# Steps of weight pieces and of tokens drawn apart, four places for small products, a shorter lag of the second product

## The chip, the cores and the metric

The kernel runs on one core of a Trainium2 chip. The core has TensorE (PE, matmuls, with its weight loads shown apart as PEld), VectorE (DVE), ScalarE (ACT), GpSimd (POOL) and SyncE (SP, which issues most DMAs). Each engine works off its own queue in order. The metric is the device time of one execution in microseconds (us); of the kernel before, three runs have a median of 1328.83 us (1327.54 to 1329.64).

## The reference

Three stages follow each other. Attention over 2 x 768 tokens with 8 heads gives 1536 rows of 512. A mixture of 8 experts sends each row to one expert. A second, dense mixture sends every row through all experts:

```python
def _moe2_ref(x, w_gate, w1, w2):          # x 1536 x 512, w1 8 x 512 x 1024, w2 8 x 1024 x 512
    logits = x @ w_gate
    logits = logits - logits.max()
    P = np.exp(logits)
    for _ in range(8):
        P /= P.sum(1, keepdims=True) + 1e-09
        P /= P.sum(0, keepdims=True) + 1e-09
        P *= N / E
    out = np.zeros((N, D), dtype=np.float32)
    for e in range(E):
        h = np.maximum(x @ w1[e], 0.0)
        out += P[:, e:e + 1] * (h @ w2[e])
```

## The kernel before

*Stages in time.* Attention ends at about 125 us of the trace, the top-1 mixture runs to about 330 us in blocks of 256 sorted rows, and the dense mixture takes the rest, from 346.86 us (its first product) on.

*The dense mixture.* There are 24 units: 8 experts times 3 groups of 512 tokens (`CHUNKS`). Both products are block products of 2 x 2 blocks that are made from 7 smaller products of sums of blocks. A number is split in a high and a low f16 part and multiplied in three matmuls. `first(u, fc, i)` (L1201) does the i-th of the seven small products of a chunk of hidden columns, 6 matmuls into one bank `fx` or `fa`; ACT takes the result (`take`, L1223) and DVE adds (L1226). When a chunk's seven are through, `operands2` (L1244) makes the second product's operands: ACT casts hh (L1256, L1268), DVE makes hl (L1259, L1271) and four sums (L1262 to L1265). `second(e, k, s, i)` (L1286) does one of its seven small products, 12 matmuls into `gx` or `ga`, and adds to the output rows `acc` (L1323, L1331, L1339).

*Weights.* An expert has 8 pieces (class `Piece`, L663): 4 of each weight. A piece is loaded in a buffer `raw` (three of them), its scale is measured (`measure`: ACT's Square with a sum, L691, and a DVE copy `sqb`, L692), PE sums it over the partitions and DVE makes a power of two of it (`rate`, L697, L627, L630), POOL makes sums of blocks (`sums` L705, `sum4` L709), and ACT and DVE write the high and low parts: `raw_hi` and `raw_lo` of the three blocks as they are, `sum_hi` and `sum_lo` of the four sums (L713, L718). The pieces of the first expert are prepared beside the blocks of the top-1 mixture, one step of the list that `plain` returns at a time.

*Tokens.* `tokens(j)` (L1027) makes the dense stage's operands for a pair of row tiles: `load`, `turn` (PE transposes, ACT copies), `operands` (L1063, four sums on DVE, five casts on ACT, five subtractions on DVE or POOL, in one go) and `logits`, a small product. `mixing` (L1098) makes the gates and the eight normalisations. Small products (the scale of a piece, logits, mixing) go to one bank of the pool `pz`.

*The order.* From the first unit on, the program's order is written out. Time is counted in ticks; a unit has 28, an expert 84. `at(tick, f)` puts a step into a plan. The loop at the end goes over the ticks, calls the steps planned for it, then a first product if one is due, and then at times a second product, as a credit in matmul columns allows, `LAG` of it behind the end of the unit. All engines get their instructions in that order. Loads, measures and rates of pieces stand at fixed distances in ticks (`load + 5`, `load + 8`, `begin + 4`).

Of the kernel before, what the change touches and what calls it, by code (L numbers as in the profile page):

```python
# [108 lines left out]
def body(ctx: ExitStack, tc: tile.TileContext, q, k, v, wg1, w1a, w2a, wg2, w1b, w2b, cst, out):  # L109
# [553 lines left out]
    class Piece:  # L663
# [23 lines left out]
        def measure(self, junk):  # L687
            o = own[id(self.raw)]; assert o is self, (self.e, self.second, self.j, o.e, o.second, o.j)
            ssq_, sqb_ = ssq[self.x][:, self.i : self.i + 1], sqb[self.x][:, self.i : self.i + 1]
# [157 lines left out]
    if True:  # L847
# [112 lines left out]
        def plain(i, p):  # L960
# [3 lines left out]
            return [lambda: p.load(raw), idle, idle, lambda: p.measure(junk), p.rate, lambda: (p.raw_hi(), p.sums()), lambda: (p.raw_lo(), p.sum4()),  # L964
# [33 lines left out]
    pz = ctx.enter_context(tc.tile_pool(name="pz", bufs=1, space=PSUM))  # L998
    ps_small.append((pz, "m"))
# [27 lines left out]
    def tokens(j):  # L1027
# [35 lines left out]
        def operands():  # L1063
            t4 = tmp[1].rearrange("p (k t) -> p k t", k=2 * KC)
            c1, c2 = ps
            b11, b21, b12, b22 = c1[:, :K2], c1[:, K2:], c2[:, :K2], c2[:, K2:]
            s1, s2, s3, s4 = (t4[:, i * K2 : (i + 1) * K2] for i in range(4))
# [4 lines left out]
            nc.vector.scalar_tensor_tensor(out=s3, in0=s2, scalar=-1.0, in1=b11, op0=ALU.mult, op1=ALU.subtract)  # L1072
            parts((T1, T2), t4[:, : 2 * K2], nc.vector)
            parts((B22,), b22, nc.vector)
            parts((T3, T4), t4[:, 2 * K2 :], nc.gpsimd if j else nc.vector)
            nc.scalar.copy(bh, b12)
# [19 lines left out]
        return load, turn, operands, logits  # L1096
# [104 lines left out]
    def first(u, fc, i):  # L1201
# [84 lines left out]
    def second(e, k, s, i):  # L1286
# [4 lines left out]
        if i == 0:  # L1291
            gs["x"] = pg.tile([P, DM], F32, tag="x", name="gx")
        if i == 1:
            gs["a"] = pg.tile([P, 2, Q], F32, tag="a", name="ga", bufs=1)
# [35 lines left out]
        if i in (2, 4) or e == E - 1:  # L1330
# [3 lines left out]
            if e == E - 1 and i in (4, 6):  # L1334
                nc.sync.dma_start(out=out[t * P : (t + 1) * P], in_=acc[:, t])
# [14 lines left out]
    pairs[0][0]()  # L1350
    pairs[1][0]()
    warm(pz, "m", 70)
    for i in (1, 2):
        pairs[0][i]()
        pairs[1][i]()
    for j, ticks in enumerate(((2,), (4,), (0, 3, 6, 20), (1, 12, 15, 24), (20, 33, 36, 48), (21, 42, 45, 52))):
        for tick, f in zip(ticks, pairs[j][-len(ticks) :]):
            at(tick, f)
    turns = [76 + t + 5 * i for i in range(8) for t in (-3, 0)]
    for tick, f in zip([52, 54, 58, 62, 66] + turns + [115], mix):  # L1360
# [5 lines left out]
    for e in range(1, E):  # L1366
        s = TICKS * CHUNKS * e
        p1, p2, level = weights(e)
        if e == 1:
            jobs += [(s - 37, p2[0], -99, True), (s - 36, p1[0], s - 15, True), (s - 32, p1[1], s - 8, True), (s - 12, p1[2], s - 1, True)]  # L1370
            jobs += [(s - 6, p1[3], s + 6, False), (s + 1, p2[1], -99, False), (s + 9, p2[3], -99, False), (s + 14, p2[2], -99, False)]
            for p, i, load, square, rate in ((p1[3], 1, -23, -19, -16), (p2[3], 0, -23, -16, -12), (p2[1], 1, -18, -13, -10), (p2[2], 0, -15, -9, -6)):
                at(s + load, lambda p=p, i=i: p.load(spare[i]))
                at(s + square, lambda p=p: p.measure(acc[:, 3].bitcast(BF16)))
                at(s + rate, p.rate)
        else:
            jobs += [(s - 70, p2[3], None, True), (s - 58, p2[0], s - 45, True), (s - 52, p2[1], s - 45, True), (s - 45, p2[2], s - 45, True)]
            jobs += [(s - 32, p1[0], s - 15, True), (s - 26, p1[3], None, True), (s - 19, p1[1], s - 8, True), (s - 13, p1[2], s - 1, True)]
# [8 lines left out]
    free = [47] * len(raws)  # L1387
    for want, p, begin, measure in sorted(jobs, key=lambda x: x[0]):
# [4 lines left out]
        if measure:  # L1393
            junk = raws[i][:, 4:6].rearrange("p a f -> p (a f)").bitcast(BF16)
            at(load + 5, lambda p=p, junk=junk: p.measure(junk))
            at(load + 8, p.rate)
            assert load + 8 <= s - 3, (p.e, p.second, p.j, load - s)
            end = load + 5
        if begin is not None:
            at(load + 6, p.sums)  # L1400
            if p.second and p.j == F2 - 1:
                last[p.e] = p
                end = s + 34
# [71 lines left out]
```

## Time and profile before

| | |
|---|---|
| median of 3 runs | 1328.83 us |
| profiled execution, and its span | 1334.16 us, 1332.4 us |
| PE, DVE, ACT, POOL busy | 1210.5, 1012.3, 853.5, 396.9 us |
| mean granted clock of PE | 0.969 |

The page's busy table is an average over three stages that differ. The span by slices of a fortieth (33 us each) shows this: a digit is the tenth of a slice in which the engine was busy, and PEclk the tenth of full speed that PE was granted:

```profile
PE   6898897998779779999999999999999999999997
DVE  6784766785586888979788787978978787886773
PEclk8898899999889999999999999999999999999999
```

The fourth to the tenth digit are the top-1 mixture, from the eleventh on it is the dense one. The busy time there is to be read stage by stage, and the waits with it.

### The profile page before, as it was taken

The page shows a single profiled execution, that of the slowest core. Times are in us where ns is not written, and L with a number is a line of the kernel's source. Part 1 is how long each engine was busy: PE and PEld are TensorE (multiplying, and loading weights), DVE is VectorE, ACT ScalarE, POOL GpSimd, SP SyncE. Part 2 cuts the span into 40 slices and gives each one's busy share as a digit, 9 for nine tenths or more (in the row PEclk, how much of TensorE's full clock was granted, in tenths as well). Part 3 has the DMA queues.
Part 4 walks back from the last instruction along what each step waited for, and adds up shares of the span by engine and source line. Part 5 has one row for each costly group of instructions (what it writes and reads, how often), then busy time and mean ns, then how long its engine had stood idle before and what let it go on. Part 6 is the DMA issues. An engine that isn't in the chain of part 4 may idle for free.

```text
span 1332.4 us, 27638 instructions
## 1 busy us (share of the span) xinstructions
PE 1210.5 (91%) x10551; PEld 1061.8 (80%) x10551; DVE 1012.3 (76%) x1793; ACT 853.5 (64%) x1599; POOL 396.9 (30%) x450
## 2 busy tenths in 40 slices
PE   6898897998779779999999999999999999999997
PEld 5776786887658668888888888888888888888886
DVE  6784766785586888979788787978978787886773
ACT  5685566665465746767776676677767767765440
POOL 4352434411212221332333242333334324331000
PEclk8898899999889999999999999999999999999999
DMA  9945776765422423343564544346445444643201
GB/s 197 207 85 177 236 252 203 229 196 166 145 86 94 124 79 104 87 128 91 132 151 108 131 118 124 92 121 151 112 127 127 121 97 109 151 112 84 76 33 48
DMA packets 176732, 173.58 MB, mean 130 GB/s; under 512 B 32768, under 2 KB 147840, under 8 KB 176208
## 3 DMA queue, kind: packets, MB, share of 16 engines
q1 hardware_dynamic: 163024, 143.75, 37.8%
q0 software_dynamic: 13568, 27.99, 10.9%
q8 instruction: 85, 1.39, 0.4%
q14 instruction: 55, 0.45, 0.1%
HBM read 136.10 MB, written 15.53 MB: 114 GB/s over the span
## 4 chain that ended last, share of the span: by engine, by line
PE 41%; DVE 11%; issue 5%; ACT 4%; POOL 2%; DVEq 0%; POOLq 0%; ACTq 0%
PE gx L1301 12%; PE fx L1216 11%; PE ga L1301 10%; PE fa L1216 8%; DVE w2l L718 2%; DVE hl L1271 2%; ACT hh L1268 2%; POOL raw L705 1%; DVE c L1263 1%; DVE w1l L718 1%; DVE hl L1259 1%; ACT w2h L713 1%; DVE c L1264 1%; DVE c L1265 1%; DVE acc L1331 1%
## 5 line engine op out<-in xcount | busy, mean ns | idle before, releaser
L1216 PEld LDWEIGHTS <-w1h 128*128 128x128 f16 x2688 | 261.0, 99 | 90.7 <-issue 56.3
L1301 PEld LDWEIGHTS <-hh 128*128 128x128 f16 x2688 | 264.7, 99 | 48.7 <-issue 16.6
L1216 PE MATMUL fx<-xh,w1h 128*128 128x256 f16 x736 | 202.3, 275 | 23.6 <-ACT c L1223 18.2
L1301 PE MATMUL gx<-w2h,hh 128*128 128x256 f16 x768 | 210.4, 274 | 10.2 <-DVE acc L1323 6.3
L705 POOL TENSOR_TENSOR raw<-raw 128x256 f32<-128x256 f32 x192 | 181.7, 960 | 103.3 <-ACT raw L691 92.3
L1301 PE MATMUL gx<-w2l,hh 128*128 128x256 f16 x768 | 210.5, 274 | 0.0
L1301 PE MATMUL gx<-w2h,hl 128*128 128x256 f16 x768 | 210.5, 274 | 0.0
L1216 PE MATMUL fx<-xl,w1h 128*128 128x256 f16 x736 | 202.7, 275 | 1.4 <-POOL xl L1061 1.4
L1216 PE MATMUL fx<-xh,w1l 128*128 128x256 f16 x736 | 202.9, 276 | 0.0
L1223 ACT ACTIVATE c<-fx,kap 128x256 f32<-128x256 f32 x288 | 131.9, 471 | 73.0 <-PE fx L1216 64.6
L1301 PE MATMUL ga<-w2h,hh 128*128 128x256 f16 x576 | 158.4, 275 | 4.9 <-DVE acc L1331 4.9
L1301 PE MATMUL ga<-w2l,hh 128*128 128x256 f16 x576 | 158.5, 275 | 0.0
L1301 PE MATMUL ga<-w2h,hl 128*128 128x256 f16 x576 | 158.4, 275 | 0.0
L1216 PE MATMUL fa<-xh,w1h 128*128 128x256 f16 x552 | 151.9, 275 | 4.4 <-ACT c L1223 4.4
L1216 PE MATMUL fa<-xl,w1h 128*128 128x256 f16 x552 | 151.8, 275 | 0.0
L1216 PE MATMUL fa<-xh,w1l 128*128 128x256 f16 x552 | 151.7, 275 | 0.0
L1216 PEld LDWEIGHTS <-w1l 128*128 128x128 f16 x1344 | 132.8, 99 | 18.6 <-issue 1.6
L1301 PEld LDWEIGHTS <-hl 128*128 128x128 f16 x1344 | 132.4, 99 | 16.1
L1271 DVE TENSOR_TENSOR hl<-c,hh 128x1024 f16<-128x1024 f32 x96 | 124.5, 1297 | 27.1 <-ACT hh L1268 27.0
L709 POOL TENSOR_TENSOR raw<-raw 128x256 f32<-128x256 f32 x64 | 58.3, 910 | 199.9 <-issue 104.4
L1268 ACT CAST hh<-c 128x1024 f16<-128x1024 f32 x96 | 99.8, 1039 | 23.2 <-DVE c L1265 22.0
L1339 ACT ACTIVATE y<-gx,pws 128x256 f32<-128x256 f32 x144 | 67.9, 472 | 69.7 <-PE gx L1301 51.1
(257 smaller groups left out, 2648.0 us busy)
## 6 DMA issues: line engine op xcount, KB each, us to landing
raw<-in_moe_w SPq DMA_DIRECT2D x64, 512.0 KB, 4.3
raw<-in_moe_w SPq DMA_DIRECT2D x228, 128.0 KB, 3.7
xh<-xohd SPq DMA_DIRECT2D x147, 128.0 KB, 2.6
xl<-xold SPq DMA_DIRECT2D x147, 128.0 KB, 2.9
acc<-y POOLq DMA_DIRECT2D x72, 256.0 KB, 4.1
raw<-in_moe_w SPq DMA_DIRECT2D x38, 256.0 KB, 3.7
vt<-in_v SPq DMA_DIRECT2D x16, 240.0 KB, 8.1
raw<-yd SPq DMA_DIRECT2D x12, 260.0 KB, 3.0
```

The costliest lines, as they stand in the source:

```text
L705: nc.gpsimd.tensor_tensor(out=r[to], in0=r[x], in1=r[y], op=ALU.add if sign > 0 else ALU.subtract)
L709: nc.gpsimd.tensor_tensor(out=self.raw[:, 2], in0=self.raw[:, 2], in1=self.raw[:, 5 if self.second else 4], op=ALU.add)
L713: nc.scalar.activation(self.dst()[0][:, w], self.raw[:, s], AF.Copy, scale=wsc[self.x][:, self.i : self.i + 1])
L718: nc.vector.scalar_tensor_tensor(out=lo[:, w], in0=self.raw[:, s], scalar=wsc[self.x][:, self.i : self.i + 1], in1=hi[:, w], op0=ALU.mult, ...
L1216: nc.tensor.matmul(p, l[:, a, kc * P : (kc + 1) * P], r[:, j, kc], start=new and kc == 0 and m == 0, stop=kc == K2 - 1 and m == 2, skip_gr ...
L1223: nc.scalar.activation(c[:, q], p, f, scale=k_)
L1259: nc.vector.scalar_tensor_tensor(out=h[1][:, :3], in0=raw, scalar=0.0, in1=h[0][:, :3], op0=ALU.max, op1=ALU.subtract)
L1263: nc.vector.tensor_tensor(out=r1, in0=r1, in1=r0, op=ALU.subtract)
L1268: nc.scalar.copy(h[0][:, 3:], c)
L1271: nc.vector.tensor_tensor(out=h[1][:, 3:], in0=c, in1=h[0][:, 3:], op=ALU.subtract)
L1301: nc.tensor.matmul(p, l, r, start=new and f == 0 and m == 0, stop=f == F2 - 1 and m == 2, skip_group_check=True)
L1339: nc.scalar.activation(gs["s"][:, d], p, AF.Copy, scale=w)
```

## The change

The change draws steps apart and moves them:

- `measure` is split. The copy `sqb` becomes `measured`, a step of its own two ticks behind the Square; `rate` stands at load + 11 (was + 8), `sums` at + 7 (was + 6), `raw_hi` not before + 13 (was + 9), `sum_hi` four ticks behind `sum4` (was two). `plain` has one step more.
- `operands` of tokens becomes seven steps (S12, P1, P2, P3, S34, P4, P5), for four of the six pairs one a tick. P1's subtraction goes from POOL to DVE.
- `pz` becomes one tile with four places that are taken in turn.
- The first two steps of mixing are called before the dense stage; its normalisations come six ticks apart, not five, from tick 66.
- A second product comes in every second tick, six ticks behind its unit; after the last first product one a tick, between the planned steps. The last unit's operands come at 12 to 16 instead of 12 to 18, and the last group uses banks of the first product's pool.
- The last expert's output goes out in pieces of half a row tile where it went in whole ones.

```diff
@@ class Piece
-            nc.scalar.activation(junk, raw, AF.Square, accum_out=ssq_)
-            nc.vector.tensor_copy(sqb_, ssq_)
+            nc.scalar.activation(junk, raw, AF.Square, accum_out=ssq[self.x][:, self.i : self.i + 1])
+
+        def measured(self):
+            i = slice(self.i, self.i + 1)
+            nc.vector.tensor_copy(sqb[self.x][:, i], ssq[self.x][:, i])
@@ plain
-            return [lambda: p.load(raw), idle, idle, lambda: p.measure(junk), p.rate, lambda: (p.raw_hi(), p.sums()), lambda: (p.raw_lo(), p.sum4()),
+            return [lambda: p.load(raw), idle, idle, lambda: p.measure(junk), p.measured, p.rate, lambda: (p.raw_hi(), p.sums()), p.raw_lo, p.sum4,
                     idle, p.sum_hi, p.sum_lo]
@@ pools
+    pzt = pz.tile([P, 4, P], F32, name="pz")
+    class Small:
+        def __init__(self):
+            self.n = itertools.count()
+        def tile(self, shape, dt, tag=None, name=None):
+            n = math.prod(shape[1:])
+            t = pzt[: shape[0], next(self.n) % 4, :n]
+            return t if len(shape) == 2 else t.rearrange("p (a b) -> p a b", a=shape[1])
+    pz = Small()
@@ tokens
-            parts((B11, B21), c1, nc.gpsimd)
+        def part1():
+            parts((B11, B21), ps[0], nc.vector)
...
+        return load, turn, sums12, part1, part2, part3, sums34, part4, part5, logits
@@ first
-            for d, f in zip((12, 13, 14, 17, 18), operands2(u, fc)):
+            for d, f in zip((12, 13, 14, 15, 16) if u == len(UNITS) - 1 and fc == F2 - 1 else (12, 13, 14, 17, 18), operands2(u, fc)):
@@ second
-            gs["a"] = pg.tile([P, 2, Q], F32, tag="a", name="ga", bufs=1)
+            late = (e, k, s) == (E - 1, CHUNKS - 1, 1)
+            gs["a"] = (pf_ if late else pg).tile([P, 2, Q], F32, tag="a", name="ga", bufs=2 if late else 1)
...
-            if e == E - 1 and i in (4, 6):
-                nc.sync.dma_start(out=out[t * P : (t + 1) * P], in_=acc[:, t])
+            if e == E - 1 and i in (4, 5, 6):
+                nc.sync.dma_start(out=out[t * P : (t + 1) * P, d], in_=to)
@@ the plan
+    for step in (TURN, P1_, S12, P2_):
+        for j in (0, 1):
+            pairs[j][step]()
+    for j in (0, 1):
+        for step, tick in ((P3_, 1), (S34, 3), (P4_, 4), (P5_, 5), (LOGITS, 13 + j)):
+            at(tick, pairs[j][step])
+    for j, load, turn in ((2, 6, 11), (3, 7, 20), (4, 20, 32), (5, 29, 42)):
...
-            at(load + 8, p.rate)
+            at(load + 7, p.measured)
+            at(load + 11, p.rate)
...
-                begin = max(begin, load + 9)
+                begin = max(begin, load + 13)
...
-                end = begin + 5
+                end = begin + 7
@@ the loop
-            if rest and (credit >= COST2 or rest[0][:2] == (0, 0)):
-                e, k, s, i = rest[0]
-                if now >= ended.get((e, k), now) + LAG:
-                    second(*rest.pop(0))
+            elif tick > max(ticks):
+                credit = 2
+            if rest and credit == 2 and tick >= ended.get(rest[0][:2], tick) + LAG - 2 * (tick > max(ticks)):
+                second(*rest.pop(0))
+                credit = 0
+            tick += 1
```

On DVE, where the operands of the fourth pair of tokens are made, this stands before; L1061 are the subtractions of `parts`, L1068 to L1072 the four sums, L1077 the last subtraction, `c` and `hl` the work of a chunk:

```order
L1265 TENSOR_TENSOR c<-c 128x256
L1068 TENSOR_TENSOR raw_1712<-raw_1711,raw_1712 128x256
L1069 SCALAR_TENSOR_TENSOR raw_1712<-raw_1711,raw_1712 128x256
L1071 TENSOR_TENSOR raw_1712<-raw_1712 128x256
L1072 SCALAR_TENSOR_TENSOR raw_1712<-raw_1712 128x256
L1061 TENSOR_TENSOR acc<-raw_1712,acc 128x4x128
L1061 TENSOR_TENSOR acc<-raw_1711,acc 128x2x128
L1077 TENSOR_TENSOR bl<-raw_1711,bh 128x256
L1271 TENSOR_TENSOR hl<-c,hh 128x1024
```

And this of the changed kernel (L1087, L1088 and L1092, L1093 are the sums, L1076 the subtractions, L1110 the last one):

```order
L1087 TENSOR_TENSOR raw_1712<-raw_1711,raw_1712 128x256
L1088 SCALAR_TENSOR_TENSOR raw_1712<-raw_1711,raw_1712 128x256
L1076 TENSOR_TENSOR acc<-raw_1712,acc 128x4x128
L1092 TENSOR_TENSOR raw_1712<-raw_1712 128x256
L1093 SCALAR_TENSOR_TENSOR raw_1712<-raw_1712 128x256
L1076 TENSOR_TENSOR acc<-raw_1712,acc 128x4x128
L1304 TENSOR_TENSOR hl<-c,hh 128x1024
L1076 TENSOR_TENSOR acc<-raw_1711,acc 128x2x128
L1259 SCALAR_TENSOR_TENSOR c<-fa,kap_1700,c 128x512
L1292 SCALAR_TENSOR_TENSOR hl<-c,hh 128x768
```

The four sums stood together, with the subtractions behind them; now two sums, a subtraction and two sums follow, and the chunk's hl and additions stand between the later subtractions. One 128x4x128 subtraction more is there: it was POOL's.

On DVE, where in a steady expert a piece is measured, this stands before (L692 is the copy sqb, L627 and L630 the rate's DVE half):

```order
L1265 TENSOR_TENSOR c<-c 128x256
L692 CAST sqb_1695<-ssq_1693 128x1
L1331 SCALAR_TENSOR_TENSOR acc<-ga,pws,acc 128x256
L627 TENSOR_SCALAR gsc_1697<-pf 128x1
L630 TENSOR_SCALAR wsc_1699<-gsc_1697 128x1
```

And this of the changed kernel (L694 is the copy, L720 a piece's low part):

```order
L720 SCALAR_TENSOR_TENSOR w2l_1687<-raw_1710,wsc_1699,w2h_1686 128x1024
L694 CAST sqb_1695<-ssq_1693 128x1
L1304 TENSOR_TENSOR hl<-c,hh 128x1024
L1365 SCALAR_TENSOR_TENSOR acc<-ga,pws,acc 128x512
L1259 SCALAR_TENSOR_TENSOR c<-fa,kap_1700,c 128x512
L1292 SCALAR_TENSOR_TENSOR hl<-c,hh 128x768
L1259 SCALAR_TENSOR_TENSOR c<-fx,kap_1700,c 128x256
L627 TENSOR_SCALAR gsc_1697<-pz 128x1
L630 TENSOR_SCALAR wsc_1699<-gsc_1697 128x1
```

One instruction stood between the copy and the rate's DVE half; now five stand there.

On DVE at the end of the program, this stands before (L1331 adds to the output rows):

```order
L1271 TENSOR_TENSOR hl<-c,hh 128x1024
L1331 SCALAR_TENSOR_TENSOR acc<-ga,pws,acc 128x256
L1331 SCALAR_TENSOR_TENSOR acc<-gx,pws,acc 128x256
L1331 SCALAR_TENSOR_TENSOR acc<-ga,pws,acc 128x512
L1331 SCALAR_TENSOR_TENSOR acc<-gx,pws,acc 128x256 x3
```

And this of the changed kernel (L1365 adds to the output rows):

```order
L1292 SCALAR_TENSOR_TENSOR hl<-c,hh 128x768
L1365 SCALAR_TENSOR_TENSOR acc<-ga,pws,acc 128x512
L1295 SCALAR_TENSOR_TENSOR c<-c 128x256
L1296 TENSOR_TENSOR c<-c 128x256
L1297 TENSOR_TENSOR c<-c 128x256
L1298 TENSOR_TENSOR c<-c 128x256
L1365 SCALAR_TENSOR_TENSOR acc<-gx,pws,acc 128x256 x2
L1304 TENSOR_TENSOR hl<-c,hh 128x1024
L1365 SCALAR_TENSOR_TENSOR acc<-gx,pws,acc 128x256
```

All additions of the last second products stood behind the last hl; now three of them stand between its four sums and ahead of it.

## Rows read from the trace of the kernel before

**Rows 1.** The page's first line.

```profile
span 1332.4 us, 27638 instructions
```

**Rows 2.** Windows: stretch, length; busy PE, PEld, DVE, ACT, POOL (instructions); clock, DMA, GB/s.

```profile
194.40:223.10 28.70, 24.58 (x155) 21.69 (x155) 20.77 (x35) 19.41 (x32) 15.43 (x13) 1.00 0.75 230
223.10:254.00 30.90, 25.81 (x154) 23.46 (x153) 21.79 (x35) 20.13 (x33) 12.96 (x12) 0.89 0.68 202
254.00:281.20 27.20, 24.20 (x156) 21.54 (x156) 20.02 (x35) 19.76 (x31) 9.77 (x9) 1.00 0.68 213
281.20:304.60 23.40, 23.40 (x154) 21.46 (x154) 17.38 (x34) 15.93 (x26) 2.67 (x4) 1.00 0.63 203
346.80:522.00 175.20, 144.25 (x1308) 123.12 (x1308) 137.73 (x296) 105.25 (x195) 39.17 (x49) 0.91 0.33 104
522.00:602.00 80.00, 75.83 (x681) 66.70 (x679) 68.02 (x114) 58.41 (x101) 26.95 (x30) 0.98 0.43 114
602.00:1179.40 577.40, 555.10 (x5071) 492.66 (x5070) 474.57 (x772) 409.23 (x702) 193.92 (x220) 1.00 0.49 121
1179.40:1332.40 153.00, 141.70 (x1260) 124.80 (x1259) 98.94 (x165) 65.52 (x110) 13.76 (x16) 0.98 0.23 65
```

**Rows 3.** Waits of PE, 350 to 522 us: us in total, times, longest.

```profile
PE fa L1216 <- ACT c L1223: 9.5, 2, 5.1
PE pf L697 <- DVE gsc L627: 7.0, 3, 4.4
PE gx L1301 <- DVE acc L1323: 6.3, 4, 3.8
```

**Rows 4.** Waits of PE, 602 to 1179 us.

```profile
PE fx L1216 <- ACT c L1223: 11.5, 14, 2.4
PE pf L697 <- DVE sqb L692: 8.8, 5, 1.8
```

**Rows 5.** Timeline, top-1 mixture: start, us, instruction, [idle before <- releaser].

```profile
226.74 1.06 ACT L691 ACTIVATE raw<-raw 128x1024 bf16<-128x1024 f32 x1 [3.55 <-DMA raw<-in_moe_w]
...
227.92 0.16 DVE L692 CAST sqb<-ssq 128x1 bf16<-128x1 f32 x1 [4.25 <-ACT raw L691]
...
232.76 0.58 PE L812 MATMUL ph<-xh,wh 128*128 128x256 f32 x1 [5.06 <-DVE hl L818]
```

**Rows 6.** Timeline of the start, and groups by form (busy, mean ns | idle).

```profile
346.89 1.66 POOL L1061 TENSOR_TENSOR xl<-x,xh 128x512 f16<-128x512 f32 x1 [0.84 <-ACT xh L1060]
...
348.61 0.37 PE L1216 MATMUL fx<-xl,w1h 128*128 128x256 f16 x1 [1.37 <-POOL xl L1061]
...
369.29 1.48 ACT L1060 CAST acc<-raw 128x512 f16<-128x512 f32 x3 [3.26 <-DVE raw L1069]
...
L1077 DVE TENSOR_TENSOR bl<-raw,bh 128x256 f16<-128x256 f32 x6 | 6.8, 1142 | 0.2
...
L1061 DVE TENSOR_TENSOR xl<-raw,xh 128x512 f16<-128x512 f32 x4 | 4.1, 1018 | 2.5 <-ACT xh L1060 2.4
...
L1061 DVE TENSOR_TENSOR acc<-raw,acc 128x256 f16<-128x256 f32 x2 | 0.8, 418 | 0.0
```

**Rows 7.** Timeline of a steady expert: a measured piece, and its boundary.

```profile
896.49 1.75 DVE L718 SCALAR_TENSOR_TENSOR w2l<-raw,wsc,w2h 128x1024 f16<-128x1024 f32 x1
898.16 0.14 DVE L692 CAST sqb<-ssq 128x1 bf16<-128x1 f32 x1
...
945.79 1.15 ACT L713 ACTIVATE w1h<-raw,wsc 128x1024 f16<-128x1024 f32 x1 [3.57 <-POOL raw L709]
```

**Rows 8.** Timeline: hl of an expert's first unit, and its use.

```profile
1004.37 1.22 DVE L1271 TENSOR_TENSOR hl<-c,hh 128x1024 f16<-128x1024 f32 x1
...
1008.99 0.27 PE L1301 MATMUL ga<-w2h,hh 128*128 128x256 f16 x1
```

**Rows 9.** Waits of PE, 1179 to 1333 us.

```profile
PE ga L1301 <- DVE acc L1331: 4.9, 1, 4.9
...
PE gx L1301 <- DVE acc L1331: 1.7, 3, 0.6
```

More of the change, by code (lines that the diff above doesn't have):

```diff
@@ L1349, in body @@
     mix = mixing()
-    pairs[0][0]()
-    pairs[1][0]()
-    warm(pz, "m", 70)
[L1353 to L1360, printed above, removed]
+    LOAD, TURN, S12, P1_, P2_, P3_, S34, P4_, P5_, LOGITS = range(10)
+    for j in (0, 1):
+        pairs[j][LOAD]()
+    mix[0]()
+    mix[1]()
+    warm(pz, "m", 70)
+    for step in (TURN, P1_, S12, P2_):
+        for j in (0, 1):
+            pairs[j][step]()
+    for j in (0, 1):
+        for step, tick in ((P3_, 1), (S34, 3), (P4_, 4), (P5_, 5), (LOGITS, 13 + j)):
+            at(tick, pairs[j][step])
+    for j, load, turn in ((2, 6, 11), (3, 7, 20), (4, 20, 32), (5, 29, 42)):
+        for step, tick in ((LOAD, load), (TURN, turn), (S12, turn + 2), (P1_, turn + 3), (S34, turn + 4), (P2_, turn + 5), (P3_, turn + 6), (P4_, turn + 7), (P5_, turn + 8), (LOGITS, turn + 11)):
+            at(tick, pairs[j][step])
+    turns = [66 + 6 * i + t for i in range(8) for t in (0, 4)]
+    for tick, f in zip([55, 58, 62] + turns + [115], mix[2:]):
         at(tick, f)
@@ L1395, in body @@
             at(load + 5, lambda p=p, junk=junk: p.measure(junk))
-            at(load + 8, p.rate)
-            assert load + 8 <= s - 3, (p.e, p.second, p.j, load - s)
+            at(load + 7, p.measured)
+            at(load + 11, p.rate)
+            assert load + 11 <= s - 3, (p.e, p.second, p.j, load - s)
             end = load + 5
         if begin is not None:
-            at(load + 6, p.sums)
+            at(load + 7, p.sums)
             if p.second and p.j == F2 - 1:
                 last[p.e] = p
-                end = s + 34
+                end = s + 37
                 assert load < s + 20, (p.e, p.second, p.j, load - s)
             else:
-                begin = max(begin, load + 9)
+                begin = max(begin, load + 13)
                 at(begin, p.raw_hi)
@@ L1425, in body @@
             rest += [(e, k, s, i) for s in range(2) for i in range(7)]
-    COST1, COST2 = 3 * K2 * 109, 3 * F2 * 109
-    LAG = 6 * (COST1 + COST2 // 2)
+    LAG = 6
     ended = {}
-    now = credit = 0
+    credit = 0
     with tc.manual_schedule():
-        for tick in range(max(ticks) + 8):
+        tick = 0
+        while rest or plan:
             for f in plan.pop(tick, ()):
@@ L1435, in body @@
                 u, fc, i = ticks[tick]
-                e, k = UNITS[u]
                 first(u, fc, i)
-                now += COST1
-                credit = min(credit + COST1, COST2)
+                credit = min(credit + 1, 2)
                 if (fc, i) == (F2 - 1, 6):
-                    ended[e, k] = now
-            if rest and (credit >= COST2 or rest[0][:2] == (0, 0)):
-                e, k, s, i = rest[0]
-                if now >= ended.get((e, k), now) + LAG:
-                    second(*rest.pop(0))
-                    credit -= COST2
-                    now += COST2
-        for x in rest:
-            second(*x)
-        rest.clear()
-    assert not plan, sorted(plan)
+                    ended[UNITS[u]] = tick
+            elif tick > max(ticks):
+                credit = 2
+            if rest and credit == 2 and tick >= ended.get(rest[0][:2], tick) + LAG - 2 * (tick > max(ticks)):
+                second(*rest.pop(0))
+                credit = 0
+            tick += 1
 _INS = ["q", "k", "v", "moe_w_gate", "moe_w1", "moe_w2", "moe2_w_gate", "moe2_w1", "moe2_w2"]
```

30 lines of the change are left out of this document (19 added, 11 removed).

## The prediction

> **What bounds the kernel now.** I read the page first [rows 1]: a span of 1332.4 us in an execution of 1334.16 us. All sums below are made against that execution; the median of the three runs, 1328.83 us, is 5.3 us lower, and I subtract the same gain from it. Then the table of stretches [rows 2], which is the view that decides: it gives, for each stretch, its length, the busy time of TensorE (PE), of its weight loads, of DVE, ACT and POOL, then the granted clock. From 602 to 1179 us, five experts of the dense stage, PE is busy 555.1 of 577.4 us at a clock of 1.00: this stretch has 22.3 us to give and no more, whatever becomes of the other engines. From 346.8 to 522 us, the start of the dense stage, PE is busy only 144.3 of 175.2 us, the granted clock is 0.91 (a mean of its two levels, 1.2 and 2.4 GHz: 18% of the stretch at the lower one), and DVE with 137.7 us is nearly as full as PE. The blocks of the first mixture (top-1) beside which weight pieces are prepared take 28.7, 30.9 and 27.2 us; the block behind them, without pieces, takes 23.4.
>
> Then the waits of PE. In the start it waits 9.5 us for ACT's first take of a chunk, 7.0 us in three places for the scale's DVE half (gsc) before a small product may use its one bank again, 6.3 us for the additions that free a bank of the second product [rows 3]. In the steady experts it waits for just two things: 11.5 us in 14 places for ACT's take, 8.8 us in 5 places for the copy sqb [rows 4]. At the end it stands 4.9 us before the second half of the last second products and 1.7 us in three more places [rows 9].
>
> **Part 1, a piece's steps drawn apart.** Steady state: sqb, a copy of 0.14 us, stands on DVE behind w2l of 1.75 us, and the rate matmul on PE follows it [rows 7]. The matmul now comes four ticks after the copy instead of three. A tick is 577.4 / 5 / 84 = 1.375 us, against a wait of 8.8 / 5 = 1.76 us, so 5 x 1.375 = 7 us go and 2 stay. Low end of this edit alone: what stands ahead of the copy on DVE grows by as much, 0. The other half of it is ACT's w1h, which stands 3.57 us idle behind POOL's last sum [rows 7], with the takes behind it: that is where the 11.5 us come from. Its distance to the sum grows from two ticks to four, +2.75 us, so 0.8 of the 3.57 is left; but the waits at the chunk heads have other causes too, and I take half, 6 us. Steady sum 13, bounds 1 (the 7 less the loss of part 4) and 20.3 (both rows of waits).
>
> In the top-1 stage: ACT stands 3.55 us idle in its Square for the weight DMA, the sqb behind it lets DVE stand 4.25 us, and PE then waits 5.06 us for DVE's hl of the block's work [rows 5]. The Square moves behind five ACT instructions of the block (two casts, two row operations, a relu), which pass while its load lands. The ceiling is 28.7 + 30.9 + 27.2 - 3 x 23.4 = 16.6 us. The pieces' own ACT, DVE and POOL work stays in the block, so I take 6; bounds -3 (the raw buffers are held one step longer, and a load that comes that much later is waited for again: nearest row, the 3.55) and +15.
>
> **Part 2, four places for small products, tokens in small steps.** The 7.0 us for gsc should go, since a small product now has three more places before it meets an unread one. Of tokens, what was one block of fourteen ACT, DVE and POOL instructions becomes seven steps a tick apart; ACT's cast stood 3.26 us behind DVE's sum in that block [rows 6], with PE's next take behind both. Six subtractions of 128x512 go from POOL to DVE, at 1.02 us each [rows 6]: +6.1 us of DVE. So DVE's work in the start is 137.7 + 6.1 = 143.8 us, and PE's is 1308 matmuls at the full clock's 0.109 us (the pace of rows 8: 555.1 us for 5071), 143 us. Two engines, equally full. The waits listed (22.8 us) and the lost clock, 0.09 x 175.2 = 15.8 us, can't all come back, because DVE would have to be busy without a gap. If the start ends with DVE at 0.82 (its share in the steady stretch, 474.6 / 577.4) it takes 175.4 us and gains nothing; at 0.87, 165.3 us, 10 gained; at 0.90, 159.8 us, 15 gained. I take 10, since PE and not DVE ends the waits in the steady stretch, so 0.82 is no ceiling. Bounds: -6 (the DVE work on top, nothing hidden) and +17.
>
> A row speaks for more: six subtractions bl of 128x256 take 1.14 us in the mean, while the same form took 0.42 in two other places [rows 6]. The Trainium skill ("SBUF — State Buffer", section "Who interferes with whom") says that a DVE instruction with two SBUF inputs and a GpSimd instruction that reads SBUF share one pair of ports, and whichever comes second is blocked for the whole of the other. By that rule six POOL subtractions fewer hand back about 6 x 0.72 = 4.3 us of DVE, an estimate from the two rows, and the start at 0.87 would gain 15 and not 10. I leave it out of the sum, since the POOL sums of the pieces remain beside DVE.
>
> The first product of the dense stage waits 1.37 us for xl, which POOL makes in 1.66 us [rows 6]. DVE makes it now, behind two sums: 2 us gained with what the earlier mixing steps take out of the way; bounds 0 and 3 (this wait and the whole 1.66 us). The two mixing steps that move ahead of the stage are seven small DVE instructions and an exponential on ACT; I price them at nothing, since they stand where attention ends and the engines wait for its last rows; without that cover they cost at the size of the copy sqb [rows 7] 7 x 0.14 = 1 us. From 522 to 602 us, with the last pair and mixing, PE is idle 4.2 us and 0.02 x 80 = 1.6 us of clock are lost: 3 gained, bounds -1 and +5.
>
> **Part 3, the end.** The last unit's operands come two ticks earlier, its second products stand between them, and its sums use another pair of banks. The 4.9 us wait for acc goes, and with it the half-clock stretch that follows it: of 0.02 x 153 = 3.1 us lost in the last window, the half, 1.5. The products come so close behind the operands that I charge one hl, 1.2 us [rows 8, 9]. 5 gained; bounds -1 (a wait for hl of the old length in place of that for acc) and 8.1 (the 1.7 as well). The six further output DMAs are issued by SP, which nothing waits for there; nothing.
>
> **Part 4, second product nearer.** From 12 ticks to 10 behind the first product's end: 2 x 1.375 = 2.75 us. In the tightest unit, the first of an expert, hl ends at 1005.59 and is used at 1008.99 [rows 8]: 3.4 us, so 0.65 stays. It is no gain by itself in the steady stretch, and no loss while DVE's hl is not over 0.65 us later there. If one w2l of 1.75 us slips ahead of each such hl, 5 x (1.75 - 0.65) = 5.5 us are lost, which is the low end above.
>
> **Sum.** Top-1 stage 6, prelude 2, start 10, 522 to 602 us 3, steady 13, end 5: 39 us. 1334.16 - 39 = 1295 for a profiled execution, 1328.83 - 39 = 1290 for the median. All low ends together (-3, 0, -6, -1, 1, -1) give 10 us slower, 1339; all high ends (15, 3, 17, 5, 20.3, 8.1) 68 us faster, 1260.
>
> **Rivals.**
> *DVE ends the start.* Then the start gains 1, the next stretch 1, the top-1 stage 1 (ACT and DVE have the same work there), the prelude 2, the steady part 11, the end 5: 21 us, 1308. For it: DVE 79% busy in a stretch where much of it is chained behind ACT; against it: the longest waits there are for single blocks, not for a queue that is always full.
> *The four places don't part.* If an instruction on one place is still held back for a reader of another, the 7.0 us for gsc stay, and the half clock behind them: the start gains 2, the sum is 31, 1298. For it: the four lie in one tile, so it rests on how accesses are told apart; against it: each place is its own range. The Trainium skill ("PSUM — Partial Sum Buffer", "PSUM bank collisions raise a hardware error") says that two engines must be kept apart by bank and quadrant, not by address; no run here shows it, and by it the four would be worth no more than the one.
> *Slower: the second product waits for hl in every unit.* Mechanism of part 4: DVE has 6.1 us more in the start, and the tokens' steps stand between a unit's sums and hl. If hl comes later than its slack, PE stands in front of the second product that is the first to use hl's sums, once in each of 24 units. The gain of 39 is eaten at 39 / 24 = 1.6 us per unit. At a wait of 3.4 us, the slack that was there before [rows 8], it costs 24 x 3.4 = 82 us, net 43 slower, 1372. For it: 0.65 us is little. Against it: only one unit in three is that tight, and the steps that DVE does for a piece are the same as before.
> *No change:* the waits only change their names, 1328.
> *All of it works:* start 17, top-1 stage 12, steady 20, the rest as above (2, 3, 5): 59 us, 1270.
>
> **Chances.** Forecast 0.56, DVE ends the start 0.22, places don't part 0.06, slower 0.07, no change 0.03, all of it 0.06. The likeliest's own range is 1276 to 1303; with the first rival and most of the high case, 1266 to 1314 holds 8 in 10. A measurement of this kernel tells about 0.2%, 2.7 us, from nothing. Faster 0.56 + 0.22 + 0.06 + 0.06 = 0.90, same 0.03, slower 0.07.
>
> **What would show it.** Right: in the steady stretch no wait of PE for sqb, and an expert in about 113 us instead of 115.5; no wait of PE for gsc in the start, DVE's share there at 0.87 or above and the start in about 165 us; the top-1 blocks with pieces near 27 us; no half clock behind 1302 us, and in the last window no wait over 2 us. Wrong: waits of PE's second product for DVE's hl (part 4), a start of 175 us with new waits of PE for DVE (first rival), gsc still named there (second rival), or blocks of 28 to 31 us with Square still waiting for its DMA. The sum is refuted above 1314 and below 1266.

## The result, and the profile after

The changed kernel takes 1290.31 us (median of 4 runs, 1288.83 to 1292.05) against 1329.24 us for the kernel before: ratio 0.9703, 95% interval 0.9675 to 0.973, 39 us less. The profiled execution took 1290.94 us, 43.2 us less than that of before (1334.16 us), which lay 5 us above its own median.

The table of stretches of the changed kernel, cut as [rows 2] is (first four units, next two, five steady experts, the rest; columns as there). Each cut stands within a microsecond of a unit's first product:

```profile
341.20:498.20 157.00, 138.53 (x1318) 120.87 (x1318) 135.31 (x293) 105.06 (x196) 36.76 (x43) 0.97 0.36 113
498.20:573.10 74.90, 73.90 (x683) 65.93 (x681) 67.36 (x125) 60.23 (x105) 28.37 (x31) 1.00 0.48 124
573.10:1145.40 572.30, 557.05 (x5083) 495.60 (x5081) 468.29 (x773) 410.59 (x703) 196.44 (x220) 0.99 0.49 123
1145.40:1289.20 143.80, 136.08 (x1240) 120.97 (x1237) 95.72 (x159) 62.84 (x106) 13.92 (x15) 1.00 0.25 69
```

With the same cuts the stretches of before are 175.0, 80.0, 579.5 and 151.0 us long. The gain lies in the start (18.0 us) more than in the long steady stretch (7.2 us); the next two units gave 5.1, the end 7.2. What is left of the 43.2 us lies ahead of the first product: 4.3 in the top-1 stage, 1.3 behind it. Of the 18 us of the start 12.4 are idle time of PE and 5.6 its busy time (144.1 us before, 138.5 now), because fewer matmuls run at the lower clock. DVE's busy time in the start is 135.3 us, less than before (137.5), although it got six subtractions more; seven small gate instructions left the stretch.

One execution differs from another: the start of the three kernels below that are all but the same there as the changed one (e2, e4, e10) took 155.3 to 157.0 us, the steady stretch of the three that are the same there (e1, e2, e8) 572.3 to 573.9. A difference of 2 us in one trace says little.

The waits of PE in the start, which answer to [rows 3]:

```profile
PE gx L1335 <- DVE acc L1357: 3.7, 2, 3.0
PE pz L699 <- DVE sqb L694: 3.5, 2, 2.3
PE fx L1249 <- ACT c L1256: 3.0, 3, 1.4
PE pz L1120 <- DVE bl L1110: 2.6, 2, 2.0
```

ACT's take before `fa` (9.5 us) and gsc (7.0 us) are gone. In the steady stretch, against [rows 4], one wait is left, and in the end two of 1 us or more:

```profile
PE fx L1249 <- ACT c L1256: 15.2, 15, 1.6
```

```profile
PE gx L1335 <- DVE acc L1365: 2.8, 3, 1.6
PE ga L1335 <- DVE acc L1365: 1.0, 1, 1.0
```

sqb is gone from the steady stretch. The waits for takes are not fewer than before: cut at the same units, 13.5 us became 15.2. They have moved, from the expert's boundary to the middle of its second-last unit. At the boundary this stood in the trace of before, around the idle ACT of [rows 7] (DVE, POOL, ACT, PE):

```profile
941.85 1.59 DVE L1262 SCALAR_TENSOR_TENSOR c<-c 128x256 f32<-128x256 f32 x1
943.47 0.83 DVE L1263 TENSOR_TENSOR c<-c 128x256 f32<-128x256 f32 x1
944.34 0.83 DVE L1264 TENSOR_TENSOR c<-c 128x256 f32<-128x256 f32 x1
945.21 0.83 DVE L1265 TENSOR_TENSOR c<-c 128x256 f32<-128x256 f32 x1
...
942.13 2.76 POOL L705 TENSOR_TENSOR raw<-raw 128x256 f32<-128x256 f32 x3
944.85 0.91 POOL L709 TENSOR_TENSOR raw<-raw 128x256 f32<-128x256 f32 x1
...
946.85 1.03 ACT L1268 CAST hh<-c 128x1024 f16<-128x1024 f32 x1
...
948.30 0.27 PE L1216 MATMUL fx<-xh,w1h 128*128 128x256 f16 x1 [2.00 <-ACT c L1223]
```

DVE's four sums are long there too, beside POOL's, and they end at 946.04. So hh could have come 0.8 us earlier at best without w1h ahead of it, where PE waits 2.0 us for the take behind it.

The timeline of the changed kernel shows the same around one of its five places; here POOL, then DVE, ACT and PE:

```profile
846.99 0.72 POOL L711 TENSOR_TENSOR raw<-raw 128x256 f32<-128x256 f32 x1 [14.07 <-issue]
...
848.40 3.29 POOL L707 TENSOR_TENSOR raw<-raw 128x256 f32<-128x256 f32 x3
...
852.22 2.78 POOL L707 TENSOR_TENSOR raw<-raw 128x256 f32<-128x256 f32 x3
...
848.15 2.09 DVE L1292 SCALAR_TENSOR_TENSOR hl<-c,hh 128x768 f16<-128x768 f32 x1
...
851.14 0.83 DVE L1296 TENSOR_TENSOR c<-c 128x256 f32<-128x256 f32 x1
852.01 1.55 DVE L1297 TENSOR_TENSOR c<-c 128x256 f32<-128x256 f32 x1
853.59 0.83 DVE L1298 TENSOR_TENSOR c<-c 128x256 f32<-128x256 f32 x1
...
854.45 1.04 ACT L1301 CAST hh<-c 128x1024 f16<-128x1024 f32 x1 [2.75 <-DVE c L1298]
855.40 0.47 ACT L1256 ACTIVATE c<-fx,kap 128x256 f32<-128x256 f32 x1
...
855.92 0.27 PE L1249 MATMUL fx<-xh,w1h 128*128 128x256 f16 x1 [1.05 <-ACT c L1256]
858.29 0.37 PE L1249 MATMUL fx<-xh,w1h 128*128 128x256 f16 x1 [1.55 <-ACT c L1256]
```

To be read from the bottom: PE waits for a take, the first take stands behind hh (the second behind a w2h besides), hh waits for DVE's four sums, and these stretch (0.83, 1.55, 0.83 us) while POOL works on two pieces' sums. In the kernel with the first piece loaded early, below, the same sums take 0.42.

### The profile page after: what moved, and what is told of

Read it like the earlier page. It is cut to its first block, busy times and chain, and to the rows that moved or that the text cites. A ratio compares the mean times of both kernels' runs of the same rounds, so it can differ in the third digit from the quotient of the medians.

```text
span 1289.2 us, 27659 instructions
## 1 busy us (share of the span) xinstructions
PE 1198.1 (93%) x10551; PEld 1055.1 (82%) x10551; DVE 995.6 (77%) x1799; ACT 852.0 (66%) x1599; POOL 396.9 (31%) x444
## 4 chain that ended last, share of the span: by engine, by line
PE 54%; DVE 11%; ACT 5%; issue 2%; DMA 2%; POOL 0%; SPq 0%; DVEq 0%; ACTq 0%
PE gx L1335 16%; PE fx L1249 15%; PE ga L1335 12%; PE fa L1249 11%; DVE hl L1292 2%; DVE c L1259 2%; ACT w2h L715 1%; ACT hh L1301 1%; DVE c L1297 1%; DVE w2l L720 1%; DMA raw<-in_moe_w 1%; DVE c L1296 1%; ACT c L1256 1%; DVE w1l L720 1%; DVE c L1298 1%
## 5 line engine op out<-in xcount | busy, mean ns | idle before, releaser
L707 POOL TENSOR_TENSOR raw<-raw 128x256 f32<-128x256 f32 x192 | 190.1, 1005 | 61.5 <-ACT raw L690 38.0
L1304 DVE TENSOR_TENSOR hl<-c,hh 128x1024 f16<-128x1024 f32 x96 | 121.0, 1261 | 62.4 <-ACT hh L1301 62.4
L711 POOL TENSOR_TENSOR raw<-raw 128x256 f32<-128x256 f32 x64 | 57.4, 896 | 292.9 <-issue 211.9
```

Of the source, the lines that this page charges most:

```text
L707: nc.gpsimd.tensor_tensor(out=r[to], in0=r[x], in1=r[y], op=ALU.add if sign > 0 else ALU.subtract)
L711: nc.gpsimd.tensor_tensor(out=self.raw[:, 2], in0=self.raw[:, 2], in1=self.raw[:, 5 if self.second else 4], op=ALU.add)
L1304: nc.vector.tensor_tensor(out=h[1][:, 3:], in0=c, in1=h[0][:, 3:], op=ALU.subtract)
```

## The experiments

Each was run on one chip beside the kernel before (medians of 1328.75 to 1331.6 us there). "After" is the changed kernel, 0.9703 of before.

**The six subtractions.** `e1_sub_on_pool`:

```diff
-            parts((B11, B21), ps[0], nc.vector)
+            parts((B11, B21), ps[0], nc.gpsimd)
```

> The changed kernel, but the six 128x512 subtractions of the tokens' first part stand on POOL again. Theory (POOL's subtractions hold DVE up while they run, so moving them to DVE gave DVE back about what it cost): DVE's busy time in the first four units of the dense stage stays at 135 +- 2 us although six instructions of 0.69 us leave it, bl is above 1.0 us in the mean again instead of 0.82, and the first four units take 157 us or up to 4 more; whole kernel 1290 to 1296 us. Rival (the sum as the prediction made it: DVE simply has less to do): DVE's busy time falls by 4.1 us to 131, the four units take about 153 us, whole kernel about 1286 us.

Measured: ratio 0.9708 (0.9688 to 0.9728), not told apart from after. The first four units in the trace:

```profile
341.70:501.50 159.80, 138.68 (x1317) 120.84 (x1317) 136.38 (x287) 105.07 (x196) 44.29 (x49) 0.97 0.35 112
```

DVE has six instructions fewer and is busy 1.1 us longer, and the stretch is 2.8 us longer. The theory's main point holds; its detail doesn't: bl stayed at 0.81 us, so bl was not what POOL's subtractions held up. By groups it was the 15 hl of 128x768 (1.01 us in the mean, here 1.13) and the 14 sums of L1296 (0.57, here 0.63).

**The four places.** `e2_one_place`: `next(self.n) % 4` became `% 1`.

> The changed kernel, but all small products take the same one of the four places. Theory (the four places are what took away PE's waits for the scale's DVE half in the start, 7.0 us, and half-clock stretches behind them): those waits are back, 5 to 8 us of them between 350 and 500 us, the first four units take 163 to 168 us instead of 157, whole kernel 1296 to 1302 us. Rival (the waits went because the steps around the small products were drawn apart; the places are worth nothing): PE's waits for gsc stay under 1 us, the four units 157 us, whole kernel 1290 us.

Measured: 0.9689 (0.9667 to 0.971), the first four units 156.9 us, no wait for gsc. The rival was right: with the steps apart the places are worth nothing that can be measured. Nor do they part the small products. In the changed kernel, with four places, the matmul of a scale stands ready (its sqb were copied at 417.51) until DVE has read the small product before it, which lies in another place:

```profile
417.51 0.19 DVE L694 CAST sqb<-ssq 128x1 bf16<-128x1 f32 x2
421.18 0.15 DVE L1173 COPY ngm<-pz 128x1 f32<-128x1 f32 x1
...
421.38 0.16 PE L699 MATMUL pz<-sqb,ones_b 128*128 128x1 bf16 x1 [0.67 <-DVE ngm L1173]
```

The same wait, 0.67 us long, stands in the trace with one place.

**The lag.** `e3_lag8`: `LAG = 6` became `LAG = 8`.

> The changed kernel with the second product eight ticks behind its unit instead of six, the distance that the steady stretch had before. Theory (the lag by itself moves no wait in the steady stretch and matters once, at the end, and a little in the start): steady stretch 572 us as it is, the last three units up to 3 us longer, whole kernel 1290 to 1294 us. Rival (the nearer second product is a term of its own, because it frees banks and operand buffers earlier): waits of PE for takes and for the bank of gx grow in every unit, over 0.4 us each, whole kernel above 1300 us.

Measured: 0.9792 (0.9749 to 0.9834). The first four units take 166.3 us, the next two 79.8, the steady stretch 570.7, the end 145.2. The wait in the start that grew:

```profile
PE gx L1335 <- DVE acc L1357: 9.9, 4, 3.1
```

Each was half right: the steady stretch doesn't mind the lag, as the theory had it, but the start does, by 9.3 us, and the next two units by 4.9. 6.2 us of the 9.3 are this wait for DVE's additions of the first expert; why they come later for PE was not traced.

**The first piece earlier.** `e4_first_sums_early`:

```diff
-            jobs += [(s - 70, p2[3], None, True), (s - 58, p2[0], s - 45, True), ...
+            jobs += [(s - 70, p2[3], None, True), (s - 62, p2[0], s - 45, True), ...
```

> The changed kernel with one number other: in experts 2 to 7 the first piece of the second weight is loaded four ticks earlier, so that POOL's three sums of it stand ahead of the queue's wait for the last piece and its DMA issue. In the changed kernel they run from 848.40 to 851.69 us beside hl (2.09 us instead of about 1.0), the next piece's sums follow at 852.22 beside DVE's four sums (0.55, 0.83, 1.55, 0.83 us instead of 0.42 each), ACT's hh waits 2.75 us for these, and PE then waits 1.05 + 1.55 + 0.46 us for takes, once in each expert. Theory (POOL beside DVE is the cause of these three waits): they shrink to under 1 us in all, the half clock near 870 and 985 us goes, whole kernel 1274 to 1282 us. Rival (ACT's own queue is the cause: a w2h of 1.13 us, a Square of 1.04 us and an hh ahead of the take): the waits stay at 3 us an expert, whole kernel 1288 to 1292 us.

Measured: 1268.21 us, 0.9518 (0.95 to 0.9536), better than expected and faster than both kernels. The steady stretch, its one wait, and DVE's sums at the same place:

```profile
575.30:1129.90 554.60, 552.19 (x5083) 493.96 (x5082) 459.08 (x773) 408.39 (x703) 197.62 (x220) 1.00 0.50 127
```

```profile
PE fx L1249 <- ACT c L1256: 2.3, 5, 0.5
```

```profile
845.49 0.42 DVE L1296 TENSOR_TENSOR c<-c 128x256 f32<-128x256 f32 x1
...
846.41 0.42 DVE L1298 TENSOR_TENSOR c<-c 128x256 f32<-128x256 f32 x1
```

PE is busy 552.2 of 554.6 us. The profiled execution (1275.37 us) was the longest of five, 7 us above the median, and its steady stretch is 17.7 us shorter than that of after, where the medians differ by 22.1; where the rest lies is open. The edit moves the load, the Square, the copy and the rate along with POOL's sums, so one more run parts these from the sums.

`e10_load_early_sums_late`, as the last, with one line more:

```diff
-            at(load + 7, p.sums)
+            at(s - 51 if p.e > 1 and p.second and p.j == 0 else load + 7, p.sums)
```

> As the kernel that loads an expert's first piece of the second weight four ticks earlier (1268.2 us), but POOL's sums of that piece are put back to the tick where the changed kernel has them; its load, ACT's Square, DVE's copy and rate stay early. Theory (POOL's sums beside DVE's hl and four sums cause the three waits for takes): the waits are back, about 3 us an expert, steady stretch near 572 us, whole kernel 1286 to 1292 us. Rival (the earlier Square, which leaves ACT's queue ahead of the takes, brought the gain): steady stretch near 555 us, whole kernel 1267 to 1272 us.

Measured: 0.9619 (0.9594 to 0.9644), between the two; steady stretch 560.7 us, 7.6 us of waits for takes. The collision is back, shorter:

```profile
841.44 3.30 POOL L707 TENSOR_TENSOR raw<-raw 128x256 f32<-128x256 f32 x3
```

```profile
841.39 1.89 DVE L1292 SCALAR_TENSOR_TENSOR hl<-c,hh 128x768 f16<-128x768 f32 x1
...
844.19 0.84 DVE L1296 TENSOR_TENSOR c<-c 128x256 f32<-128x256 f32 x1
...
846.63 1.04 ACT L1301 CAST hh<-c 128x1024 f16<-128x1024 f32 x1 [0.88 <-DVE c L1298]
```

Of the 17.7 us that the steady stretch gained with the earlier piece, 6.1 hang on where POOL's sums stand (560.7 to 554.6) and 11.6 on the earlier load, Square, copy and rate (572.3 to 560.7), which no run parts. Neither theory alone. The medians, 9.3 us apart, give the sums' place more than 6.1. As for the 11.6, in the changed kernel the Square stands ahead of the chunk's hh on ACT, so w2h, w2l and POOL's last sum of the piece before, which waits for w2l, come about a microsecond later in the unit (POOL's L711 starts 9.55 us into it, 8.40 here), and POOL's sums then fall fully on DVE's four sums. That the 11.6 us go through this chain is argued, not shown.

**The rate.** `e6_rate_back`:

```diff
-            at(load + 7, p.measured)
-            at(load + 11, p.rate)
+            at(load + 5, p.measured)
+            at(load + 8, p.rate)
```

> The changed kernel, but in the dense stage the copy sqb stands in the Square's tick again (load + 5) and the rate at load + 8; all else as changed. Theory (the two ticks between Square and copy and the fourth tick before the rate took away PE's waits for sqb): 1.3 to 1.8 us an expert are back behind sqb, steady stretch 579 to 582 us, whole kernel 1298 to 1302 us. Rival (other moves, of w2l above all, cleared DVE's queue ahead of the copy): no wait for sqb over 0.4 us in the steady stretch, whole kernel 1288 to 1292 us.

Measured: 0.9863 (0.9839 to 0.9887), some 21 us lost, more than the theory said. The steady stretch is 586.4 us, and PE's longest wait there:

```profile
PE pz L699 <- DVE sqb L694: 16.4, 5, 3.3
```

A wait is 3.3 us here and was 1.8 in the kernel before. The copy stands behind the four sums and a w2l, and the sums are stretched by POOL, as in the changed kernel:

```profile
868.44 1.54 DVE L1297 TENSOR_TENSOR c<-c 128x256 f32<-128x256 f32 x1
...
872.44 0.14 DVE L694 CAST sqb<-ssq 128x1 bf16<-128x1 f32 x1
...
872.63 0.16 PE L699 MATMUL pz<-sqb,ones_b 128*128 128x1 bf16 x1 [3.28 <-DVE sqb L694]
```

The waits for takes shrink to 2.2 us in exchange, and 3.6 us for ga's additions are new. Of the 14.1 us that the stretch lost, 6.9 are idle time of PE and 7.2 busy time (564.3 against 557.1 us for the same matmuls), that is, matmuls at the lower clock.

The start lost 10.2 us as well: a wait of 4.2 us for sqb and one of 4.2 us for gsc stand in it, the latter with four places.

**Tokens in one block.** `e8_tokens_block`: all seven steps of a pair's operands at `turn + 3`.

> The changed kernel, but the seven steps of the operands of the last four pairs of tokens stand in one tick (turn + 3) as they did before, the subtraction still on DVE. Theory (the spreading keeps PE's takes out of a queue of casts; the prediction put most of the start's gain here): PE waits again some 3 to 5 us for a take at two of the four pairs, with a half-clock stretch behind each, the first four units take 165 to 170 us instead of 157, whole kernel 1298 to 1303 us. Rival (the nearer second product gave the start its time; the kernel with the lag of eight ticks lost 9.2 us there): 157 to 160 us, whole kernel 1290 to 1293 us.

Measured: 0.9781 (0.9763 to 0.9798). The first four units take 165.6 us, 8.6 more, behind the takes:

```profile
PE fx L1249 <- ACT c L1256: 9.3, 6, 3.0
...
PE fa L1249 <- ACT c L1256: 3.3, 1, 3.3
```

The theory was right.

**The new loop alone on the kernel before.** `e12_before_new_loop`: the loop as in the change (LAG, credit, one second product a tick at the end), nothing else.

> The kernel before with one part of the change alone: the loop at the end that sets the second products (every second tick, six ticks behind the unit, one a tick after the last first product). Theory (the nearer second product is a term of the first six units, worth the 9 + 5 us that the lag of eight ticks lost): first four units 163 to 168 us instead of 175, next two 75 to 78 instead of 80, steady stretch as before (579), whole kernel 1310 to 1318 us. Rival (it is worth something only together with the steps drawn apart, since before the start's waits are behind ACT's casts): the six units gain under 4 us, whole kernel 1324 to 1330 us.

Measured: 0.9883 (0.9864 to 0.9903), about 15 us gained, but at other places than the theory said: the first four units 174.0 us and the next two 78.4, that is 2.6 us together; the steady stretch 572.1 us, 7.4 gained; the end 145.3, 5.7 gained. In the steady stretch:

```profile
PE ga L1301 <- DVE acc L1331: 11.7, 10, 1.3
...
PE pf L697 <- DVE sqb L692: 1.7, 5, 0.3
PE fx L1216 <- ACT c L1223: 0.5, 1, 0.5
```

Of the 22.3 us of both old waits 2.2 are left by the place of the second products alone, and a new one, for ga's additions, takes more than half of the gain back.

**The pieces' steps alone on the kernel before.** `e13_before_pieces_apart`: `measured`, the distances and the jobs of the change, in the dense stage only.

> The kernel before with another part of the change alone: the weight pieces' steps in the dense stage (copy two ticks behind the Square, rate at load + 11, sums at + 7, raw_hi not before + 13, sum_hi four ticks behind sum4, the jobs' new wants); loop, tokens, places, top-1 stage and end as before. Theory (the prediction's: drawing these steps apart takes away 7 of the 8.8 us for sqb and half of the waits for takes): no wait for sqb over 0.5 us in the steady stretch, stretch 564 to 568 us instead of 579.5, whole kernel 1312 to 1320 us. Rival (the new loop alone had already taken the steady stretch to 572.1 us and the waits for sqb to 1.7 us, so the place of the second products decides and the pieces' steps alone give nothing): steady stretch 577 us or more with new waits for takes, whole kernel 1325 to 1332 us.

Measured: 0.9954 (0.9935 to 0.9973). The steady stretch takes 570.6 us, 8.9 less, with no wait for sqb, but:

```profile
PE fx L1218 <- ACT c L1225: 16.5, 15, 1.7
```

sqb as the theory had it, the takes as the rival had it. The first four units take 175.8 us against 175.0: no gain.

**The last sums near.** `e7_sum4_near`: `end = begin + 7` became `end = begin + 5`.

> The changed kernel, but sum_hi and sum_lo stand two ticks behind POOL's sum4 again instead of four. Theory (the prediction's: ACT's w1h idles behind POOL's sum and holds the takes up, once at each expert's end): waits of about 2 us for a take are back at each expert's first unit, steady stretch 580 us or more, whole kernel 1297 to 1303 us. Rival (in the kernel before with the new loop alone, which has the two ticks, these waits were 0.5 us in all; the distance is worth nothing): steady stretch within 2 us of 572, whole kernel 1288 to 1293 us.

Measured: 0.9817 (0.9787 to 0.9848), steady stretch 579.5 us. The size is near the theory's, the wait is not: takes 13.7 us, not more than in after, but new in the experts' first units

```profile
PE ga L1335 <- DVE acc L1365: 7.4, 5, 1.7
```

**The top-1 stage.** `e5_plain_back`: the old list of steps in `plain`.

> The changed kernel, but the steps of the pieces beside the top-1 blocks are those of before (copy in the Square's step, raw_hi with sums, raw_lo with sum4). Theory (the Square stood in front of the block's ACT work and waited there for its DMA): waits of PE for DVE's hl of 2 to 5 us are back, the top-1 stage takes 190 to 192 us instead of 187, whole kernel 1293 to 1297 us. Rival (the 4.3 us came from the spread of loads over the blocks or from noise of half-clock stretches): 186 to 188 us, whole kernel 1289 to 1292 us.

Measured: 0.9724 (0.9699 to 0.9749), top-1 stage 187.0 us against 186.9 of after. The theory's size fell: with the old list of steps the stage took 186.4 to 191.2 us in four traces, with the new one 184.1 to 187.8 in ten. Its wait is real: with the old list PE waits 4.6 us for DVE's hl in one block, with the new one no longer. But from block to block, the blocks with pieces take 27.6, 30.6 and 26.8 us with the old list, and 28.5, 28.4 and 25.5 with the new one, and the block behind them 23.4 and 26.7. What the wait gave is lost one block later; why was not tried.

**The start once more.** `e11_early_and_start`, on the kernel with the early piece: logits at `turn + 12`, rates of the four spare pieces one to two ticks later.

> The kernel with the earlier first piece (1268.2 us) and two more distances in the start: the rate of the four pieces that are measured in spare space comes one to two ticks later behind its copy, the logits one tick later behind bl. In its trace PE waits 1.19 and 2.34 us for sqb at the ticks 73 and 77 and 0.56 and 1.99 us for bl at the ticks 21 and 30. Theory (the same rule as in the steady stretch: a small product needs four ticks behind its DVE step, or PE stands): these 6 us of waits go, the first four units take 150 to 153 us instead of 157, whole kernel 1260 to 1265 us. Rival (DVE is full in the start at 0.86, so the wait only moves to the next product): 156 to 158 us, whole kernel 1266 to 1270 us.

Measured: 0.9556 (0.9531 to 0.9582). In its profile the first four units take 154.0 us, 3 less; in the runs that isn't seen, the interval overlaps that of the early piece (0.95 to 0.9536) by a hair and its median is higher. Inconclusive.

## Why the prediction was right, and which of its steps were not

The total was right: 39 us forecast, 39 measured in the medians. Several terms were not, and the errors cancelled; that the sum came out to the microsecond is luck.

- *Top-1 stage*, forecast 6: nothing that can be told from the scatter between traces. The step that failed is that a wait gone is time gained: the Square's stall in [rows 5] and PE's wait behind it went, and the block behind the pieces got 3.3 us longer.
- *Prelude*, forecast 2: 1.3 (18.8 to 17.5 us from the top-1 stage's last matmul to the first product).
- *Start*, forecast 10, measured 18. The share of DVE was right (0.87 forecast, 135.3 / 157.0 = 0.86), its work was wrong: 143.8 us forecast, 135.3 measured. The subtractions were priced at the mean of [rows 6], 1.02 us, which holds collisions; in the changed kernel the group that answers to it reads (busy, mean ns)

```profile
L1076 DVE TENSOR_TENSOR xl<-raw,xh 128x512 f16<-128x512 f32 x7 | 4.8, 686 | 4.2 <-ACT xh L1075 4.2
```

  that is 0.69 us, 2 us less for the six. The gate steps that left the stretch took 2 us along, which I hadn't credited, and the six bl fell from 1.14 to 0.82 us in the mean, another 2. The prediction told of a rule by which the gain would be 15, of POOL and DVE sharing ports, and left it out. The first experiment bears out its direction (DVE not less busy with six subtractions less), but not the row that its size was taken from: with the subtractions back on POOL, bl stays as short.
- *Which edit made the start*: the prediction named the four places and the tokens' steps. The places gave nothing. The tokens' steps are worth 8.6 us there, the lag 9.3, the rate's distance 10.2, each measured by undoing it. They don't add up to 18: with the loop alone the start gains 1 us, with the pieces' steps alone nothing. The tokens' steps alone on the kernel before, and the two mixing steps that moved ahead, were not run. My reading is that PE's queue is held up by whichever step is still close.
- *Part 4, second product nearer*: the prediction gave it no gain in the steady stretch and no term elsewhere. Undone, the steady stretch indeed loses nothing, but the first six units lose 14 us: the term left at nothing in the start is the step that failed. What it claimed of hl held: no wait of PE for hl is in the dense stage's trace.
- *Steady*, forecast 13, measured 7.2. The 8.8 us for sqb went whole (7 forecast); the loop alone leaves 1.7 of it, the pieces' steps alone none. The half of the takes' waits (6) did not go: 13.5 us became 15.2. The step took ACT's idle time behind POOL's last sum for the cause. The rows of before shown above say otherwise: DVE's sums, which hh needs, were held up beside POOL's and ended only 0.25 us after w1h began. With the last sum apart, POOL's sums fall beside DVE's in another unit. The ceiling of 22.3 us was wrong too: the kernel with the early piece is 24.9 us shorter there than before, since PE's busy time, which counts matmuls at the lower clock in full, fell as well, from 557.2 to 552.2 us.
- *End*, forecast 5, measured 7.2. The loop alone gives 5.7; if the parts add, the operands, the banks and the output DMAs have 1.5. The one hl that was charged, 1.2 us, is in no wait there.
- *The rivals.* DVE did not end the start. The second product never waited for hl. The second rival was right in its mechanism: the places don't part. It was wrong in its price: the 7.0 us for gsc went all the same, because the small products now stand further from their neighbours, and came back in part (4.2 us) when the rate was put near.

The pace of 0.109 us for a matmul, which the prediction credits to rows 8, is worked out from rows 2.

What stays open is how the 11.6 us of the earlier load, Square, copy and rate split among these, and which parts of the start's gain need each other.

## What to carry to other kernels

When steps are put further apart, look where the step that was moved now falls: on the same engine beside whom, and on another engine against which two-input instructions. Price an instruction by its shortest row of the same shape, and look up who runs beside the long ones. An edit that gives little alone can be worth much when its neighbour's wait is gone (the loop in the start: 1 us added alone, 9.3 us when its lag is undone): undo parts from the full change as well as adding them to the old kernel, and expect the two lists to disagree. And when a timeline names an engine as idle, look at what the instruction behind it would have waited for next.

## What the runs showed of the hardware

A sum of 128x256 with both inputs in SBUF took DVE 0.42 us, and 0.83 or 1.55 us while POOL ran its own sums of that size (0.9 to 1.1 us each). The Trainium skill ("SBUF — State Buffer", section "Who interferes with whom") has a rule for such pairs, an exclusive lock on the ports that they share, and the two kernels that differ only in where POOL's sums stand agree that they hold each other up: hl 1.89 against 0.95 us, the sum 0.84 against 0.42, 6.1 us in five experts. Which POOL instruction held which one of DVE can't be read from the rows.

In the changed kernel the five steady experts have the same three waits of PE for takes (1.05, 1.55 and 0.46 us in the one shown). In two of the five, PE's clock is granted at the lower of its two levels (1.2 of 2.4 GHz) for a while behind the second wait: from 858.3 to 861 us the granted clock is 0.50 to 0.52, the matmul at 858.29 takes 0.37 us and those behind it 0.42, where the one at 855.92 takes 0.27. These two experts took 115.4 us, the others 113.8 or 113.9. The same waits thus bring the lower clock in one expert and not in another. A wait is at times worth more than its own length: with the early piece 17.7 us came back in the steady stretch for 12.9 us of waits (15.2 less 2.3), and the other 4.9 are busy time of PE (557.1 to 552.2 us for the same number of matmuls).
